# Moving weight loads, useless matmuls and small VectorE steps in the opening chain of a delta-rule attention with a gated MLP

## The chip, the core and the metric

The kernel runs on one core of a Trainium2 chip. The engines are TensorE (PE, with its weight loads shown as PEld), VectorE (DVE), ScalarE (ACT), GpSimd (POOL) and SyncE (SP, which issues the DMAs here). The metric is the device time of one execution in microseconds (us), as the median of several runs.

## The reference

Two parts follow each other. The first is a delta-rule attention with 4 batches, 8 heads, 768 tokens and 48 dimensions a head. Each of the 32 units keeps a 48 x 48 state, which every token reads and changes:

```python
k_n = k / (np.linalg.norm(k, axis=-1, keepdims=True) + 1e-06)
for t in range(S):
    kt, vt, bt = (k_n[:, :, t], v[:, :, t], beta[:, :, t, None])
    y[:, :, t] = np.einsum('bhd,bhde->bhe', q[:, :, t], state)
    v_old = np.einsum('bhde,bhd->bhe', state, kt)
    state = state + bt[:, :, :, None] * np.einsum('bhd,bhe->bhde', kt, vt - v_old)
```

The second is a gated MLP on the 3072 tokens, with 384 model dimensions and 1536 hidden ones: `sigmoid(x @ w_gate) * (x @ w_val) @ w_out`. All is float32.

## The kernel before

**Chunks.** The 768 tokens are worked in 12 chunks (g = 0 to 11) of 64 tokens, all 32 units at once, so a chunk gives 256 rows to the MLP. In a chunk the token-by-token recurrence becomes a triangular system: Gram matrices of k (`gram`), the norms of k from their diagonal (`norms`, 18 small DVE steps), the inverse of the triangular blocks (`solve_halves` for chunks 0 to 2, some 40 small DVE steps), products of q and k under a mask (`masked`), and then, in three steps, the new values (`updates(g, 0..2)`). In step 0 PE forms pu, and ACT and DVE copy it to su; step 1 adds to pk on PE, and `less` subtracts pk from the values on DVE (line 457); step 2 is like step 0. `rows` makes the chunk's outputs yy and copies them to ys, `flip` transposes them to xx for the MLP, and `advance` changes the state.

**The MLP.** Its hidden dimension is cut into 12 tiles (f). A slot is half a tile: in an even slot `gate_val` (line 583 for chunk 0) puts gate and value products of one tile into one of two PSUM buffers called gv, and `gated` frees it again (ACT's sigmoid, line 591, and DVE's product, line 592); in odd slots `outp` (line 611) works on the tile two before. The 36 weight pieces of 384 KB come in the order in which chunk 0 needs them: gate and value of tile 0, then for each further tile its gate and value and the output piece of the tile before. A piece n is loaded as two words a weight (`load_piece`, line 172), changed in place by two ACT instructions (`scaled`, lines 189 and 191), and joined to float32 by one on DVE (`join`, line 203). When `scaled(n)` is done, piece n + BEHIND is loaded, from piece EAGER = 14 on; the pieces before are issued by `stage`.

**The order** is written out by hand: each engine works in the order in which the program issues, and SP issues DMAs in that order too, so that a load which waits holds back those behind it. Ahead of slot 0 the program spells out the opening chain of chunk 0, in which nothing of the MLP can run. In the slots two tables, `plan` and `late`, say what is issued ahead of and behind a slot's own work. Piece 13 and piece 14 are scaled in slot 0, ahead of tile 0's sigmoid.

**Useless matmuls.** `busy_array` (line 99) issues matmuls of 128 x 512 in bf16 whose result nobody reads. In `solve_halves` of chunk 0, those at `pz` wait each for one of DVE's solving steps (`beats`); others stand between the chain's products under the names early, pm and gap.

Of the kernel before, what the change touches and what calls it, by code (L numbers as in the profile page):

```python
# [12 lines left out]
F32 = mybir.dt.float32  # L13
# [6 lines left out]
ALU = mybir.AluOpType  # L20
# [4 lines left out]
C = 64  # L25
# [5 lines left out]
J = 8  # L31
# [24 lines left out]
def deltanet_gated_mlp(ctx: ExitStack, tc: tile.TileContext, kd, qd, kv, beta, words, out):  # L56
# [39 lines left out]
    def busy_array(out, n, after=()):  # L96

        for i in range(n):
            ins = nc.tensor.matmul(out=out.rearrange("q a b -> q (a b)"), lhsT=flat[:, 0:128], rhs=flat, start=True, stop=True)
            if i < len(after):  # L100
                pace(ins, after[i])

    def load_k(g):
        for e in range(2):
            nc.sync.dma_start(kqp[g % 2][64 * e:64 * e + D, 0:2].rearrange("p s c t -> p (s c t)"), kd[g, e])

    def load_q(g, after=None):
        for e in range(2):
            ins = nc.sync.dma_start(kqp[g % 2][64 * e:64 * e + 64, 2 + e:4 + e].rearrange("p s c t -> p (s c t)"), qd[g, e])
            pace(ins, after)  # L110

    def load_rows(g, part):

        st = state[g]
        if "kv" not in st:
            st["kv"] = wk.tile([128, 2, CP, D], F32, name=f"kv_{g}", tag="kv", bufs=2)
        nc.sync.dma_start(st["kv"][:, part].rearrange("p c d -> p (c d)"), kv[g, :, part * CP * D:(part + 1) * CP * D])
        if part:
            st["beta"] = wk.tile([128, 32], F32, name=f"beta_{g}", tag="beta", bufs=2)
            nc.sync.dma_start(st["beta"], beta[:, g])  # L120
# [54 lines left out]
    def stage(lo, hi, after=None):  # L175
        for n in range(lo, hi):
            load_piece(n, after)
# [177 lines left out]
    def lower_left(g):  # L355

        if g == 0:
            for r in range(4):
                q, o = slice(32 * r, 32 * r + 32), 32 * (r % 2)
                nc.scalar.activation(wide[q, :, o:o + 16].rearrange("q c t -> q t c"), state[g]["G"][q, 0:16], AF.Copy, scale=under[q])  # L360
            return
        a = joints[g][:, 0]
        return nc.scalar.activation(a[:, :, 0:16].rearrange("q c t -> q t c"), state[g]["G"][:, 0:16], AF.Copy, scale=under)
# [9 lines left out]
    def solve_halves(g):  # L373


        st = state[g]
        gp, gam = st["gp"], st["gam"]
        X = st["X"]
        hg = wk.tile([128, 768], F32, name=f"hg_{g}", tag="hg", bufs=1)
        H = hg[:, 0:256].rearrange("q (b k t) -> q b k t", b=2, k=8)  # L380
        gs = hg[:, 256:768].rearrange("q (b i t) -> q b i t", b=2, i=16)
        for b in range(2):
            nc.vector.tensor_tensor(out=H[:, b], in0=dmask[:, 8 * b:8 * b + 8, 16 * b:16 * b + 16],
                                    in1=gam[:, 16 * b:16 * b + 16].unsqueeze(1).to_broadcast([128, 8, 16]), op=ALU.mult)
            yield
            nc.vector.scalar_tensor_tensor(out=gs[:, b], in0=gp[:, 16 * b:16 * b + 16, 16 * b:16 * b + 16], scalar=-1.0,
                                           in1=gam[:, 16 * b:16 * b + 16].unsqueeze(1).to_broadcast([128, 16, 16]), op0=ALU.mult, op1=ALU.mult)
            yield
        for j in range(15, 0, -1):
            k, n = j // 2, 8 - j // 2  # L390
            tmp = wk.tile([128, 2, n, j], F32, name=f"tmp_{g}_{j}", tag="tmp", bufs=2)
            beat(nc.vector.tensor_tensor(out=tmp, in0=H[:, :, k:8, j:j + 1].to_broadcast([128, 2, n, j]),
                                         in1=gs[:, :, j:j + 1, 0:j].to_broadcast([128, 2, n, j]), op=ALU.mult))
            yield
            beat(nc.vector.tensor_tensor(out=H[:, :, k:8, 0:j], in0=H[:, :, k:8, 0:j], in1=tmp, op=ALU.add))
            yield
        for b in range(2):
            nc.vector.tensor_copy(out=X[:, 8 * b:8 * b + 8, 16 * b:16 * b + 16], in_=H[:, b])
            yield
        A, D, Z = (joints[g][:, i] for i in range(3))  # L400
        nc.vector.transpose(mt.rearrange("q c (k r) -> q k c r", r=2), X.rearrange("q k (c r) -> q k c r", r=2))
        yield
        pool, tag = (ps_aux, "aux") if g else (ps_gv, "gv")
        pz, pm = (pool.tile([128, CP, 32], F32, name=f"{n}_{g}", tag=tag) for n in ("pz", "pm"))

        def blocks(out, lhsT, rhs):
            for c in range(CP):
                for r in range(0, 128, 32):
                    nc.tensor.matmul(out=out[r:r + 32, c], lhsT=lhsT[r:r + 32, c], rhs=rhs[r:r + 32, c], start=True, stop=True)  # L409
        if g == 0:  # L410
            paced = beats[8::2]
            busy_array(pz, len(paced) + 4, after=paced)
        if g:
            blocks(pz, A, mt)
        else:
            for c in range(CP):
                for r in range(0, 128, 64):
                    nc.tensor.matmul(out=pz[r:r + 64, c], lhsT=wide[r:r + 64, c], rhs=mt[r:r + 64, c], start=True, stop=True)
        if g == 0:
            busy_array(pm, 2)  # L420
        yield
        nc.vector.transpose(D.rearrange("q c t -> q (c t)"), mt.rearrange("q c t -> q (c t)"))
        nc.scalar.copy(Z, pz)
        yield
        blocks(pm, D, Z)
        if g == 0:
            gap.append(ps_gv.tile([128, J, C], F32, name="gap", tag="gv"))
            busy_array(gap[0], 3)
        yield
        st["joint"] = nc.vector.tensor_tensor(out=mt, in0=mt, in1=pm, op=ALU.subtract)  # L430
        yield
# [22 lines left out]
    def less(g):  # L454
        st = state[g]
        for e in range(2):
            nc.vector.tensor_tensor(out=st["R"][e], in0=st["kv"][:, 1, e * J:(e + 1) * J], in1=st["pk"][e], op=ALU.subtract)  # L457

    def updates(g, step):

        st = state[g]
        R, L = st["R"], st["L"]

        at = {(e, x): [tokens_at(e, x) + 32 * (k ^ e) for k in range(2)] for e, x in KINDS}
        if step == 1:
            for j in range(J):
                for e, x in KINDS:
                    one, two = at[e, x]
                    nc.tensor.matmul(out=st["pk"][e][two:two + 32, j], lhsT=L[one:one + 32, e * J + j], rhs=su[one:one + 32, 3 if x else e, j],  # L469
                                     start=False, stop=True, skip_group_check=True)  # L470
            less(g)
            return
        pu = [ps_aux.tile([128, J, D], F32, name=f"pu_{g}_{step}_{x}", tag="aux") for x in range(1 if g else 2)]
        for j in range(J):
            for e, x in KINDS:
                r = at[e, x][step // 2]
                nc.tensor.matmul(out=pu[0 if g else x][r:r + 32, j], lhsT=mt[r:r + 32, e * J + j], rhs=R[e][r:r + 32, j], start=True, stop=True)  # L477
        for e, x in KINDS:
            r = at[e, x][step // 2]
            if g == 0 and x:  # L480
                nc.vector.tensor_copy(out=su[r:r + 32, 3 if x else e], in_=pu[1][r:r + 32])
            else:
                nc.scalar.copy(su[r:r + 32, 3 if x else e], pu[0][r:r + 32])  # L483
# [168 lines left out]
    def take(gen, n=1):  # L652
        for _ in range(n):
            next(gen, None)
# [5 lines left out]
    scalings = [scale_v(g) for g in range(N)]  # L660
    NORMS, SOLVE, HALVES = 18, 66, 40
    joins, splits = joining(), splitting()
    EAGER, BEHIND = 14, 6


    EN = mybir.EngineType
# [12 lines left out]
    take(gram(0), 10)  # L679
    rest(0)  # L680
    masks0 = masked(0)
    gap.append(ps_gv.tile([128, J, C], F32, name="early", tag="gv"))
    busy_array(gap.pop(), 12)
    for n in range(2):
        scaled(n)
    for _ in norms(0):
# [8 lines left out]
        scaled(n)  # L695
    take(norms1, 11)
    take(halves0, 2)
    stage(10, 12, state[0]["joint"])
    load_q(1, state[0]["joint"])
    clear(1)  # L700
    take(masks0, 2)
    updates(0, 0)
    busy_array(gap[0], 5)
    stage(12, 14, lower_left(1))
    load_rows(1, 0)
    load_k(2)
    for n in range(6, 9):
        scaled(n)
    take(masks0, 2)
    updates(0, 1)  # L710
    busy_array(gap[0], 4)
    take(norms1, NORMS)
    updates(0, 2)
    busy_array(gap[0], 5)
    for n in range(9, 11):
        scaled(n)
    take(joins, 2)
    take(halves1, 4)
    rows(0)
    busy_array(gap[0], 2)  # L720
    for n in range(11, 13):
# [6 lines left out]
    for n, at in enumerate((0, 0, 1, 2, 3, 5, 6, 8, 9, 10, 10, 11, 11, 12, 12, 13, 14, 15, 16, 16, 17, 18, 18), 13):  # L728
        plan[at].append(lambda n=n: scaled(n))
    spread(joins, len(pieces) - 4, 0, 20)  # L730
    for at, n in ((0, 8), (1, 4), (2, 6), (3, 4), (4, 5), (5, 5), (6, 1), (9, 1), (11, 1)):
        plan[at].append(steps(halves1, n))
    plan[10].insert(0, steps(halves1))
    late[10].append(steps(halves1))
# [147 lines left out]
```

## Time and profile before

| | us |
|---|---|
| median of 3 runs | 636.92 (636.85 to 637.29) |
| the profiled execution | 635.61 |
| its span, first to last instruction | 633.9 |
| PE busy in the span | 614.6 |
| DVE busy | 476.8 |
| ACT busy | 344.0 |
| first gate product of tile 0 begins (line 583) | 42.09 |

The span is that of the instructions in the trace; 1.7 us of the execution lie around it. Times within the trace count from the start of the span. Where a row has an engine's name with a q, it is the engine's sequencer, which issues DMAs or waits; in the rows of stretches the last three numbers are the granted clock of TensorE, the busy share of the DMA engines and what these moved in GB/s.

### The profile page before, as it was taken

Reading aid. Unit: us, or ns where it says so; the run is one execution under the profiler, and the core shown is the slowest. Engines: PE = TensorE matmul, PEld = TensorE weight load, DVE = VectorE, ACT = ScalarE, POOL = GpSimd, SP = SyncE. Lnnn points to the kernel's source line nnn. Section 1 sums busy time; section 2 is a strip of 40 time slices with the busy share of each in tenths; the row PEclk is TensorE's granted clock in tenths of the full one; section 3 lists DMA queues with packets and bytes.
Section 4 is the critical chain, followed back from the end, with each engine's and each line's share of the span. In section 5 each row is a group of like instructions: output and inputs, shape, how many; then the busy total and the mean of one; then the engine's idle time right before and its main releaser. Section 6 shows DMA issues by size and latency. Waiting matters only on the chain.

```text
span 633.9 us, 24057 instructions
## 1 busy us (share of the span) xinstructions
PE 614.6 (97%) x10494; PEld 571.2 (90%) x10502; DVE 476.8 (75%) x1443; ACT 344.0 (54%) x933; POOL 39.6 (6%) x102
## 2 busy tenths in 40 slices
PE   6689999999999999999999999999999999999996
PEld 4367778989999999999999999999999999999996
DVE  5888897589977977977977977977987977953221
ACT  4879865567356356356355355355455455445222
POOL 6000000000002002002002002002002002001000
PEclk9999999999999999999999999999999999999999
DMA  9495831202203203103102102102112100100101
GB/s 271 177 296 181 277 91 54 53 2 87 52 3 86 52 4 86 42 12 86 45 11 86 34 21 87 27 28 86 26 29 86 26 4 3 26 3 2 26 1 25
DMA packets 17769, 41.06 MB, mean 65 GB/s; under 512 B 4224, under 2 KB 7296, under 8 KB 17664
## 3 DMA queue, kind: packets, MB, share of 16 engines
q1 hardware_dynamic: 17664, 39.53, 21.5%
q8 instruction: 82, 1.34, 0.9%
q14 instruction: 23, 0.19, 0.1%
HBM read 34.80 MB, written 4.72 MB: 62 GB/s over the span
## 4 chain that ended last, share of the span: by engine, by line
PE 91%; DVE 5%; ACT 1%; issue 1%; DMA 1%; ACTq 0%; SPq 0%; DVEq 0%
PE gv L586 45%; PE po L617 22%; PE gv L583 5%; PE pu L477 3%; PE po L611 3%; PE yy L503 2%; PE yy L506 2%; PE pk L446 2%; PE pg L291 2%; PE pp L319 2%; PE pd L524 2%; PE pk L469 1%; PE pm L409 1%; ACT su L483 1%; DVE kqp L324 1%
## 5 line engine op out<-in xcount | busy, mean ns | idle before, releaser
L586 PE MATMUL gv<-xx,w 128*128 128x256 f32 x2376 | 311.2, 285 | 0.0
L586 PEld LDWEIGHTS gv<-xx,w 128*128 128x128 f32 x2376 | 298.8, 191 | 3.1
L617 PE MATMUL po<-w,h 128*128 128x384 f32 x792 | 161.9, 340 | 0.0
L617 PEld LDWEIGHTS po<-w,h 128*128 128x128 f32 x792 | 133.8, 188 | 0.8
L597 ACT CAST h<-sg 128x256 fp32r<-128x256 f32 x132 | 53.5, 405 | 120.1 <-DVE sg L592 119.0
L591 ACT ACTIVATE sg<-gv 128x256 f32<-128x256 f32 x144 | 54.7, 380 | 107.8 <-PE gv L586 98.5
L592 DVE TENSOR_TENSOR sg<-sg,gv 128x256 f32<-128x256 f32 x144 | 60.1, 417 | 67.3 <-ACT sg L591 66.5
L350 DVE TENSOR_TENSOR X<-X,tmp 128x126 f32<-128x126 f32 (+22 forms) x279 | 71.1, 255 | 8.3
L347 DVE TENSOR_TENSOR tmp<-X,gp 128x126 f32<-128x126 f32 (+22 forms) x279 | 71.0, 254 | 8.3
L602 DVE TENSOR_TENSOR h<-sg,h 128x256 fp32r<-128x256 f32 x132 | 56.4, 428 | 13.2 <-ACT h L597 13.2
L562 POOL COPY x<-yt 32x192 f32<-32x192 f32 x72 | 28.3, 393 | 450.3 <-DVE yt L557 447.6
L279 ACT ACTIVATE kv<-kv,mq 128x48 f32<-128x48 f32 x192 | 47.9, 324 | 0.0
L483 ACT COPY su<-pu 32x384 f32<-32x384 f32 x92 | 43.3, 470 | 5.9 <-PE pu L477 4.1
L583 PE MATMUL gv<-xx,u 128*128 128x256 f32 x144 | 33.8, 385 | 0.7 <-issue 0.4
L324 DVE TENSOR_TENSOR kqp<-pp,pmask 64x512 f32<-64x512 f32 x48 | 32.3, 687 | 2.1 <-PE pp L319 1.1
L303 ACT COPY G<-pg 32x256 f32<-32x256 f32 (+1 forms) x69 | 25.3, 367 | 14.0 <-PE pg L291 12.7
L583 PEld LDWEIGHTS gv<-xx,u 128*128 128x128 f32 x144 | 26.6, 190 | 5.8 <-issue 0.8
L557 DVE STREAM_TRANSPOSE yt<-ys 128x768 f32<-128x768 f32 x9 | 8.8, 979 | 25.4 <-ACT ys L512 25.4
L457 DVE TENSOR_TENSOR R<-kv,pk 128x384 f32<-128x384 f32 x44 | 22.3, 549 | 6.6 <-PE pk L469 6.5
L562 ACT COPY x<-yt 32x192 f32<-32x192 f32 x72 | 25.2, 349 | 1.2
L212 ACT CAST w<-u 128x384 fp32r<-128x384 f32 x36 | 18.0, 508 | 8.1 <-DVE w L219 8.0
L531 DVE TENSOR_TENSOR su<-su,pd 48x384 f32<-48x384 f32 x40 | 21.7, 543 | 0.8 <-PE pd L524 0.4
(109 smaller groups left out, 556.2 us busy)
## 6 DMA issues: line engine op xcount, KB each, us to landing
raw<-in_words_dram SPq DMA_DIRECT2D x36, 384.0 KB, 5.5
kv<-in_kv_dram SPq DMA_DIRECT2D x24, 384.0 KB, 4.5
kqp<-in_qd_dram SPq DMA_DIRECT2D x24, 256.0 KB, 4.1
kqp<-in_kd_dram SPq DMA_DIRECT2D x24, 192.0 KB, 3.5
out_dram<-ot SPq DMA_DIRECT2D x48, 96.0 KB, 2.2
beta<-in_beta_dram SPq DMA_DIRECT2D x12, 16.0 KB, 4.0
```

The source lines that it names most:

```text
L279: nc.scalar.activation(V[:, c], V[:, c], AF.Copy, scale=mq[:, c, 0:1])
L347: nc.vector.tensor_tensor(out=tmp, in0=X[:, k:16, j:j + 1].to_broadcast([128, n, j]), in1=gp[:, j:j + 1, 0:j].to_broadcast([128, n, j]), o ...
L350: nc.vector.tensor_tensor(out=X[:, k:16, 0:j], in0=X[:, k:16, 0:j], in1=tmp, op=ALU.add)
L483: nc.scalar.copy(su[r:r + 32, 3 if x else e], pu[0][r:r + 32])
L562: copy(x[32 * q:32 * q + 32, :, :, a].rearrange("q k c s -> q c k s"), yt[32 * a:32 * a + 32, :, q::4])
L583: nc.tensor.matmul(out=pg[:, o], lhsT=parts[w, f][:, k * 128:(k + 1) * 128], rhs=x[0][:, k], start=k == 0, stop=k == KC - 1)
L586: nc.tensor.matmul(out=pg[:, o], lhsT=parts[w, f][:, a, k * 128:(k + 1) * 128], rhs=x[b][:, k], start=(k == 0 and q == 0), stop=(k == KC - ...
L591: nc.scalar.activation(h, st["gv", f][:, 0], AF.Sigmoid)
L592: nc.vector.tensor_tensor(out=h, in0=h, in1=st["gv", f][:, 1], op=ALU.mult)
L597: nc.scalar.copy(hh[:, 0], st["sg", f])
L602: nc.vector.tensor_tensor(out=hh[:, 1], in0=st["sg", f], in1=hh[:, 0].bitcast(F32), op=ALU.subtract)
L617: nc.tensor.matmul(out=po[s], lhsT=hh[:, a, ts], rhs=parts["o", f][:, w], start=(f == 0 and q == 0), stop=(f == NF - 1 and q == 2))
```

## The change

Six things are done at once, all ahead of slot 4 of the MLP:

- The 12 useless matmuls "early" go, four of those at pz, and one of two at pm.
- Pieces 10 to 13 are issued together when the subtraction of `updates(0, 1)` is done. Before, 10 and 11 waited for the subtraction of mt in `solve_halves` (line 430), and 12 and 13 for the ACT instruction of `lower_left(1)` (line 363). The k of chunk 2, the q of chunk 1 and the k rows of chunk 1 follow them.
- BEHIND is 5 instead of 6, so piece 14 follows `scaled(9)`.
- The second pair of chunk 0's masks stands behind the subtraction of `updates(0, 1)` instead of ahead of it, and the rest of chunk 1's norms behind the copies of `updates(0, 2)`.
- The joins of pieces 0 and 1 stand ahead of the first copies to su, instead of behind `updates(0, 2)`.
- The first four steps of `solve_halves` of chunk 1 are no longer ahead of `rows(0)`; slots 1, 2 and 3 take 6, 7 and 5 steps for 4, 6 and 4.

```diff
         if g == 0:
             paced = beats[8::2]
-            busy_array(pz, len(paced) + 4, after=paced)
+            busy_array(pz, len(paced), after=paced)
...
         if g == 0:
-            busy_array(pm, 2)
+            busy_array(pm, 1)
...
     def less(g):
         st = state[g]
         for e in range(2):
-            nc.vector.tensor_tensor(out=st["R"][e], in0=st["kv"][:, 1, e * J:(e + 1) * J], in1=st["pk"][e], op=ALU.subtract)
+            last = nc.vector.tensor_tensor(out=st["R"][e], in0=st["kv"][:, 1, e * J:(e + 1) * J], in1=st["pk"][e], op=ALU.subtract)
+        return last
...
-            less(g)
-            return
+            return less(g)
...
-    EAGER, BEHIND = 14, 6
+    EAGER, BEHIND = 14, 5
...
     masks0 = masked(0)
-    gap.append(ps_gv.tile([128, J, C], F32, name="early", tag="gv"))
-    busy_array(gap.pop(), 12)
     for n in range(2):
         scaled(n)
...
     take(halves0, 2)
-    stage(10, 12, state[0]["joint"])
-    load_q(1, state[0]["joint"])
     clear(1)
     take(masks0, 2)
+    take(joins, 2)
     updates(0, 0)
     busy_array(gap[0], 5)
-    stage(12, 14, lower_left(1))
-    load_rows(1, 0)
-    load_k(2)
+    lower_left(1)
     for n in range(6, 9):
         scaled(n)
+    stage(10, 14, updates(0, 1))
+    load_k(2)
+    load_q(1)
+    load_rows(1, 0)
+    busy_array(gap[0], 4)
     take(masks0, 2)
-    updates(0, 1)
-    busy_array(gap[0], 4)
-    take(norms1, NORMS)
     updates(0, 2)
     busy_array(gap[0], 5)
+    take(norms1, NORMS)
     for n in range(9, 11):
         scaled(n)
-    take(joins, 2)
-    take(halves1, 4)
     rows(0)
...
-    for at, n in ((0, 8), (1, 4), (2, 6), (3, 4), (4, 5), (5, 5), (6, 1), (9, 1), (11, 1)):
+    for at, n in ((0, 8), (1, 6), (2, 7), (3, 5), (4, 5), (5, 5), (6, 1), (9, 1), (11, 1)):
```

SP's queue from piece 10 to piece 14 before (raw_552 and raw_554 are pieces 10 and 11, raw_606 and raw_608 are 12 and 13, raw_619 is 14; kqp_77 takes the q of chunk 1, kqp_76 the k of chunk 2, kv_113 the k rows of chunk 1):

```order
L172 DMA raw_552<-in_words_dram 128x768
L172 DMA raw_554<-in_words_dram 128x768
L109 DMA kqp_77<-in_qd_dram 64x1024 x2
L172 DMA raw_606<-in_words_dram 128x768
L172 DMA raw_608<-in_words_dram 128x768
L117 DMA kv_113<-in_kv_dram 128x768
L105 DMA kqp_76<-in_kd_dram 48x1024 x2
L172 DMA raw_619<-in_words_dram 128x768
```

And now (raw_625 to raw_631 are pieces 10 to 13, raw_698 is piece 14):

```order
L172 DMA raw_625<-in_words_dram 128x768
L172 DMA raw_627<-in_words_dram 128x768
L172 DMA raw_629<-in_words_dram 128x768
L172 DMA raw_631<-in_words_dram 128x768
L105 DMA kqp_76<-in_kd_dram 48x1024 x2
L109 DMA kqp_77<-in_qd_dram 64x1024 x2
L117 DMA kv_113<-in_kv_dram 128x768
L172 DMA raw_698<-in_words_dram 128x768
```

The same nine transfers stand ahead of piece 14; the four pieces come first among them, and all of them stand behind one wait.

DVE from the subtraction of mt (line 430) on, before (L324 are the masks, L481 the copies to su, L457 is the subtraction in `less`, L259 a step of the norms):

```order
L430 TENSOR_TENSOR mt<-mt,pm_406 128x512
L324 TENSOR_TENSOR kqp_76<-pp_0_208,pmask 64x512 x2
L481 COPY su<-pu_0_1_563 32x384 x2
L324 TENSOR_TENSOR kqp_76<-pp_1_209,pmask 64x512 x2
L457 TENSOR_TENSOR kv_92<-kv_92,pk_0_204 128x384
L457 TENSOR_TENSOR kv_92<-kv_92,pk_1_205 128x384
L259 TENSOR_TENSOR nt_470<-nt_470,gp_466 128x32
```

And now (L203 are the joins of pieces 0 and 1):

```order
L430 TENSOR_TENSOR mt<-mt,pm_393 128x512
L324 TENSOR_TENSOR kqp_76<-pp_0_208,pmask 64x512 x2
L203 SCALAR_TENSOR_TENSOR u_538<-raw_98 128x384
L203 SCALAR_TENSOR_TENSOR u_538<-raw_100 128x384
L481 COPY su<-pu_0_1_542 32x384 x2
L457 TENSOR_TENSOR kv_92<-kv_92,pk_0_204 128x384
L457 TENSOR_TENSOR kv_92<-kv_92,pk_1_205 128x384
L324 TENSOR_TENSOR kqp_76<-pp_1_209,pmask 64x512 x2
L481 COPY su<-pu_2_1_645 32x384 x2
```

Two joins stand ahead of the first copies to su, and the second pair of masks and the norms stand behind the subtraction and the second copies.

## The prediction

> **What bounds the kernel now.** I read the page first, the shares of the chain that ended last by engine:
>
> ```profile
> PE 91%; DVE 5%; ACT 1%; issue 1%; DMA 1%; ACTq 0%; SPq 0%; DVEq 0%
> ```
>
> PE is the bound for nearly all of the span. So the change can act in two ways: it moves the moment when PE starts its dense work, or it makes PE wait after that. Then I read the same chain in order of time (start, length, what).
>
> ```profile
> 23.80 2.07 PE pz L418 x64
> ...
> 26.53 1.50 PE pm L409 x100
> ...
> 28.82 0.86 PE pu L477 x59
> 29.68 1.31 issue
> ...
> 42.09 5.42 PE gv L583 x24
> ...
> 49.33 2.79 PE gv L583 x12
> ...
> 53.40 2.59 PE gv L583 x12
> ...
> 71.22 0.42 issue
> ```
>
> Up to 42.09 us a serial chain of the first chunk passes between DVE, PE and ACT. From 42.09 on the chain is PE alone: tiles 0 and 1 of the gate and value products (24 matmuls), tile 2 at 49.33, tile 3 at 53.40. The row at 29.68 is a stall of 1.31 us inside 64 small matmuls, with nothing to wait for.
>
> **The stall in pu.** It is an instruction fetch, as three rows of the page bear out.
>
> ```profile
> PE 614.6 (97%) x10494; PEld 571.2 (90%) x10502; DVE 476.8 (75%) x1443; ACT 344.0 (54%) x933; POOL 39.6 (6%) x102
> q8 instruction: 82, 1.34, 0.9%
> ```
>
> 10494 and 10502 instructions of PE over 82 packets are 256 a packet. In program order (an f32 matmul is two loads and two multiplies) the stalls at 29.68 and 71.22 stand 1536 instructions apart, six times 256. So a block can be late when PE uses 256 instructions fast: here pm and pu, some 375 in 3 us.
>
> By the Trainium skill, "Runtime: NRT & Kernel Launch", section "Instruction fetch mechanics", blocks are indeed 256 instructions, but fetch is hidden; by that rule the shift below would be worth nothing. The 1.31 us row disagrees.
>
> The change takes 34 PE instructions out ahead of this place (12 + 4 + 1 useless matmuls of two each). The block's end moves 34 further on: out of pu, 14 instructions into pk (L469). PE reaches pk only when the su copies are done, so the block has landed by then. The block before it now ends some 34 instructions deeper in pm, and its fetch is asked for later: 0 to 0.55 us of stall there; I take 0.2, since the 32 instructions that delay the request are handed on faster than they execute.
>
> **What DVE does with that.** DVE's rows in order of time:
>
> ```profile
> 28.08 0.69 DVE L430 TENSOR_TENSOR mt<-mt,pm 128x512 f32<-128x512 f32 x1 [0.23 <-PE pm L409]
> 28.80 1.39 DVE L324 TENSOR_TENSOR kqp<-pp,pmask 64x512 f32<-64x512 f32 x2
> 31.32 1.14 DVE L481 COPY su<-pu 32x384 f32<-32x384 f32 x2 [1.13 <-PE pu L477]
> 32.49 1.40 DVE L324 TENSOR_TENSOR kqp<-pp,pmask 64x512 f32<-64x512 f32 x2
> 33.92 1.02 DVE L457 TENSOR_TENSOR kv<-kv,pk 128x384 f32<-128x384 f32 x2
> ...
> 36.50 1.14 DVE L481 COPY su<-pu 32x384 f32<-32x384 f32 x2
> 37.67 1.03 DVE L203 SCALAR_TENSOR_TENSOR u<-raw 128x384 uint32<-128x384 uint32 x2
> ```
>
> and PE's row between them:
>
> ```profile
> 32.39 0.99 PE L469 MATMUL pk<-su,L 32*32 32x48 f32 x64
> ```
>
> The change puts two word joins (1.03) behind the first two masks. The stall that leaves pu was the cover of just that slot (1.13 idle). So: subtraction of mt ends 28.97, masks 30.36, joins 31.4, su copies 32.55 (before 32.46): nothing gained so far. Then pk ends at 33.5, and the subtraction L457 starts there instead of behind two more masks (33.92): it ends at 34.6, against 34.94. The masks follow, 1.40, and the next su copies start at 36.0 instead of 36.50, since the norms' seven steps have moved behind them. The block setup of chunk 1 no longer stands ahead of the ys copy. ACT's last copy of xx waits for pieces 10 to 12, so the first gv matmul comes at 41.6: **-0.5 us** for the chain (bounds -0.75, by DVE alone, and +0.3, if piece 12 lands 0.8 late). The useless matmuls taken out of this stretch were not in it: pz waits for DVE's mt and pm for ACT's copy.
>
> **What the loads cost.** Here is SP's own order before (start, length of the issues):
>
> ```profile
> 28.79 1.00 SPq L172 DMA_DIRECT2D raw<-in_words_dram  x2
> 29.84 1.11 SPq L109 DMA_DIRECT2D kqp<-in_qd_dram  x2
> 33.02 1.39 SPq L172 DMA_DIRECT2D raw<-in_words_dram  x2
> 34.45 0.44 SPq L117 DMA_DIRECT2D kv<-in_kv_dram  x1
> 34.98 0.85 SPq L105 DMA_DIRECT2D kqp<-in_kd_dram  x2
> 35.92 19.10 SPq L172 DMA_DIRECT2D raw<-in_words_dram  x11
> ```
>
> and what waits for the first of those eleven, piece 14:
>
> ```profile
> 44.99 0.56 ACT L189 ACTIVATE raw<-raw 128x384 int32<-128x384 uint16 x1 [2.35 <-DMA raw<-in_words_dram]
> ...
> 45.89 0.36 ACT L591 ACTIVATE sg<-gv 128x256 f32<-128x256 f32 x1
> 46.28 0.42 DVE L592 TENSOR_TENSOR sg<-sg,gv 128x256 f32<-128x256 f32 x1 [1.65 <-ACT sg L591]
> ...
> 47.35 0.23 DVE L395 TENSOR_TENSOR hg<-hg,tmp 128x66 f32<-128x66 f32 x1
> 47.61 0.22 DVE L392 TENSOR_TENSOR tmp<-hg 128x60 f32<-128x60 f32 x1
> ...
> 50.41 0.42 DVE L592 TENSOR_TENSOR sg<-sg,gv 128x256 f32<-128x256 f32 x1
> ```
>
> On ACT the scaling of piece 14 stands ahead of the first sigmoid. ACT waits 2.35 us for its landing at 44.99; the gated product of tile 0 ends at 46.70, 1.71 later, that of tile 1 at 50.83, DVE having worked without a break between them (4.13). These free the two PSUM buffers for tiles 2 and 3, which PE starts at 49.33 and 53.40. So before there are 2.6 us of slack in both, and that is what hides the loads.
>
> The same nine transfers stand ahead of piece 14 after the change, but the first is issued at 34.6 instead of 28.79: 5.8 us later, for data of which ACT was already short. What gives some back is the order: four pieces together, then the narrow transfers. The answer on the word loads from 28 to 50 us has the time from issue to landing, and the stretches have the rates (last number, GB/s; DMA share ahead of it):
>
> ```profile
> DMA to landing us min/median/max: 3.0/5.4/9.0
> 10.00:15.00 5.00, 4.67 (x35) 1.88 (x33) 4.49 (x22) 2.38 (x6) 0.96 (x4) 1.00 1.04 314
> 15.00:20.00 5.00, 2.60 (x69) 1.36 (x62) 4.31 (x21) 4.77 (x11) 0.00 (x0) 1.00 1.04 398
> 37.00:41.00 4.00, 2.99 (x71) 2.42 (x72) 3.91 (x11) 3.57 (x9) 0.00 (x0) 1.00 0.95 230
> ```
>
> Piece 10 lands 3.0 after its issue (the smallest landing), at 37.6. Pieces 11 to 13, 1.18 MB at the 398 of pure pieces: 40.6. Then k, q, kv and piece 14, 1.70 MB, at the 230 of the stretch that carried such transfers before: 48.0. Ends: 46.0, with the 314 of the early mixture for the second part; 50.8, with the 218 GB/s that all nine had before (2.88 MB from 31.8 to 44.99). I take 48.0, nearest to the same transfers beside the same engines' work.
>
> From there: tile 0's product ends at 49.7, and tile 2 starts at 49.8 (+0.5). DVE then has three more steps of the next chunk's solve ahead of tile 1's product (13 for 10, one each 0.25 us: 4.13 + 0.75 = 4.9), which ends at 54.6: tile 3 at **54.7, +1.3 us** against 53.40. At the ends of the landing: -0.5 (then the chain's gain decides) and +4.1. Behind tile 3 the later products have their slack again (they keep the distance to ACT and DVE, which run without a break there), and PE does not make up lost time. So this +1.3 takes the place of the -0.5; they are not added.
>
> **The rest.** The fetch stall of 0.42 at 71.22 goes: its block end moves from the tile-6 matmuls into pu of chunk 1, behind the next output product. The following block then ends near the close of chunk 1's masks and can be late by up to 0.5: together -0.3 (-0.6 to +0.2). Pieces behind 14 come one scaling later; the late ones lay 2 to 6 us in hand, so nothing. SP's queue holds the later inputs of chunk 2 in the same places.
>
> **Sum:** 1.3 - 0.3 = +1.0 us. The profiled execution took 635.61 (span 633.9 and 1.7 around it), which makes 636.6; the median of the runs is 1.31 above that execution, so I carry the difference over: 636.92 + 1.0 = **637.9 us**.
>
> **Rivals.** (1) *The transfers run cleanly* and piece 14 lands by 46: the chain's gain stays, -0.5 - 0.3, **636.1**, down to 635.1 with the best ends. For it: 398 GB/s when pieces run alone. Against: 230 in the same place before. It decides below a landing of 46.2. (2) *A cold array.* The useless matmuls show two speeds (smallest, median and largest ns; first and last start):
>
> ```profile
> L99 PE MATMUL pz<-dmask x14: 379/389/390, 17.8 to 23.1; 128*128 128x512 bf16 x14
> L99 PE MATMUL early<-dmask x11: 379/634/634, 10.6 to 14.5; 128*128 128x512 bf16 x11
> 4.92 1.98 PE L291 MATMUL pg<-kqp 48*64 48x64 f32 x62 [0.59 <-DMA kqp<-in_kd_dram]
> 14.76 1.16 PE L291 MATMUL pg<-kqp 48*64 48x64 f32 x64
> ```
>
> The array sped up while "early" ran; 5.4 us of small matmuls before that had not done it. Without "early" it falls to the eleven paced ones, one per 0.5 us from 17.78. If these don't suffice, pz runs 1.98/1.16 x 64/62 = 1.76 times as long, +1.6, and if the array stays slow to 42 us, pz, pm, pu and pk alone (5.4 us by the rows above) cost +4.1, and what follows, as an estimate, 2 more. With a part of the loads' cost: **639.5 to 645, 642** in the middle. For: nothing dense is left before 17.8. Against: at a slow length of 0.634, with starts 0.39 apart as in "early" (ten in 3.9 us), the paced ones, one each half microsecond, still fill some 80% of 4.9 us. The Trainium skill, "TensorE: Matmul & The Clock Gate", Part 1, says that the clock is released after one busy window of about 3.4 us, and that the windows are not tied to the start of the kernel; by it the eleven would do in most executions, not in all. The rows of "early", slow at first and fast within 3.9 us, agree. (3) *Nothing moves*: landing near 47, and losses and gains cancel, **636.9**.
>
> **Chances.** Forecast 0.52 (637.0 to 640.5), rival 1 0.22, rival 2 0.13, rival 3 0.13. A measurement of this kernel tells about 0.2%, 1.3 us, from no change. Slower by more, over 638.2: three fifths of the forecast, whose bounds reach further up than down, and rival 2 whole, 0.44. Faster by more: two thirds of rival 1, with what I may have missed in the chain, 0.15. Within: 0.41. The range reaches into rival 1 and the cheap half of rival 2: 635.4 to 641.5.
>
> **What would show it.** Right: no stall in pu; subtraction L457 ends near 34.6; ACT waits 5 us or more ahead of the first sigmoid; PE idle ahead of tiles 2 and 3; none at tile 6. Wrong: piece 14 landing before 46.5, PE without a break from 42 us on, or useless matmuls of 634 ns late in the pz group.

## The result, and the profile after

The change made the kernel slower: **639.81 us** (median of 6 runs, 639.12 to 640.66) against 636.70 (median of 6 runs beside them, 635.33 to 637.29); ratio 1.0061, 95% interval 1.0049 to 1.0073. Ratios here leave disturbed runs out and so need not be the quotient of the medians. The profiled execution after took 640.00 us (span 638.3), the one before 635.61 (633.9): the two profiles differ by 4.4 us, the medians by 3.1, and the steps below are read from the profiles.

The shares of the chain that ended last, after:

```profile
PE 85%; DVE 3%; ACT 3%; DMA 1%; issue 1%; SPq 1%; ACTq 0%
```

Before, PE had 91% and ACT 1%. What has come in stands in the same chain in order of time (start, length, what):

```profile
36.19 0.33 SPq L172
...
40.77 9.37 DMA raw<-in_words_dram
...
50.17 0.56 ACT raw L189
...
53.91 0.46 ACT raw L191
54.36 0.35 ACT su L529
...
64.06 0.39 ACT sg L591
...
64.81 1.49 DVE u L203 x3
...
70.67 0.72 DVE scratch L422
...
71.52 1.28 PE pm L409 x80
```

Piece 10 is issued at 36.19 and piece 14 at 40.77; it lands at 50.15. From there the chain lies on ACT's queue for 14 us, then on DVE's, and reaches PE only at 71.52, in the pm product of chunk 1's solve (`solve_halves(1)`). PE's rows in order of time, after:

```profile
23.80 3.60 PE L418 MATMUL pz<-mt,wide 64*64 64x32 f32 x64 [1.14 <-DVE mt L401]
...
28.07 1.93 PE L409 MATMUL pm<-scratch 32*32 32x32 f32 x128
...
31.04 0.88 PE L477 MATMUL pu<-kv,mt 32*32 32x48 f32 x64
...
43.42 5.45 PE L583 MATMUL gv<-xx,u 128*128 128x256 f32 x24 [0.87 <-ACT xx L545]
...
51.93 2.86 PE L583 MATMUL gv<-xx,u 128*128 128x256 f32 x12 [1.25 <-DVE sg L592]
...
56.76 2.86 PE L583 MATMUL gv<-xx,u 128*128 128x256 f32 x12 [0.68 <-DVE sg L592]
...
71.52 1.28 PE L409 MATMUL pm<-scratch 32*32 32x32 f32 x128 [1.38 <-DVE scratch L422]
...
74.12 2.75 PE L583 MATMUL gv<-xx,u 128*128 128x256 f32 x12
```

and tile 3 and the last of these places before:

```profile
53.24 2.75 PE L583 MATMUL gv<-xx,u 128*128 128x256 f32 x12
...
66.38 1.62 PE L409 MATMUL pm<-scratch 32*32 32x32 f32 x128
...
69.33 1.89 PE L583 MATMUL gv<-xx,u 128*128 128x256 f32 x8
71.64 1.13 PE L583 MATMUL gv<-xx,u 128*128 128x256 f32 x4 [0.42 <-issue]
```

So PE is behind by 1.33 us at tile 0 (42.09 before), by 3.5 at tile 3 (53.24 in this view before), and by **5.1** at chunk 1's pm, for which it now waits 1.38; tile 6 then takes 2.75 instead of 3.44 without its fetch stall, and 4.4 are left at the end. The stall in pu is gone: 0.88 in one row at 31.04. On DVE the subtraction L457 ends at 36.17, and ACT waits 5.24 us for piece 14:

```profile
35.15 1.02 DVE L457 TENSOR_TENSOR kv<-kv,pk 128x384 f32<-128x384 f32 x2 [0.98 <-issue]
50.17 0.56 ACT L189 ACTIVATE raw<-raw 128x384 int32<-128x384 uint16 x1 [5.24 <-DMA raw<-in_words_dram]
```

And pz took 3.60 us for 2.06, under a halved clock (stretches; the columns that matter are PE busy, and at the end the granted clock, DMA share and GB/s):

```profile
20.45:23.86 3.41, 1.96 (x9) 0.52 (x9) 2.95 (x13) 3.39 (x15) 0.09 (x1) 1.00 0.47 179
23.86:30.69 6.83, 6.70 (x195) 5.58 (x196) 4.26 (x13) 4.10 (x12) 0.44 (x1) 0.50 0.02 5
```

Two causes were on the table at once, then: late words, and the half-speed stretch of rival 2.

### The profile page after: what moved, and what is told of

Its sections match the earlier page's. It is cut to its first block, busy times and chain, and to the rows that moved or that the text cites. A ratio compares the mean times of both kernels' runs of the same rounds, so it can differ in the third digit from the quotient of the medians.

```text
span 638.3 us, 24030 instructions
## 1 busy us (share of the span) xinstructions
PE 615.4 (96%) x10485; PEld 572.5 (90%) x10485; DVE 476.9 (75%) x1443; ACT 344.3 (54%) x933; POOL 39.6 (6%) x102
## 4 chain that ended last, share of the span: by engine, by line
PE 85%; DVE 3%; ACT 3%; DMA 1%; issue 1%; SPq 1%; ACTq 0%
PE gv L586 44%; PE po L617 21%; PE gv L583 3%; PE pu L477 3%; PE po L611 2%; PE yy L503 2%; PE yy L506 2%; PE pp L319 2%; PE pk L446 2%; DMA raw<-in_words_dram 1%; PE pg L291 1%; PE pd L524 1%; PE pk L470 1%; ACT su L483 1%; ACT raw L189 0%
## 5 line engine op out<-in xcount | busy, mean ns | idle before, releaser
L602 DVE TENSOR_TENSOR h<-sg,h 128x256 fp32r<-128x256 f32 x132 | 56.4, 428 | 13.2 <-ACT h L597 13.2
L324 DVE TENSOR_TENSOR kqp<-pp,pmask 64x512 f32<-64x512 f32 x48 | 32.3, 686 | 2.0 <-PE pp L319 1.1
L457 DVE TENSOR_TENSOR R<-kv,pk 128x384 f32<-128x384 f32 x44 | 22.3, 549 | 6.4 <-PE pk L470 6.4
L189 ACT ACTIVATE raw<-raw 128x384 int32<-128x384 uint16 x36 | 20.0, 557 | 7.0 <-DMA raw<-in_words_dram 7.0
L291 PE MATMUL pg<-kqp 48*64 48x64 f32 x768 | 16.2, 235 | 7.8 <-DMA kqp<-in_kd_dram 7.8
```

Source lines behind the costliest of these rows:

```text
L602: nc.vector.tensor_tensor(out=hh[:, 1], in0=st["sg", f], in1=hh[:, 0].bitcast(F32), op=ALU.subtract)
```

## The experiments

The theories, as the expectations use them. **A**: the moment at which the words land costs; ACT's and DVE's in-order queues carry the lateness to PE. **B**: the half-speed array costs. **C**: the new order of joins, masks and norms on DVE costs. Each ratio below is against the kernel before on the same chip (medians there 635.4 to 636.0).

### One of the three parts undone, or done alone

`loads_back`, after with the loads of before:

```diff
+    stage(10, 12, state[0]["joint"])
+    load_q(1, state[0]["joint"])
...
+    stage(12, 14, lower_left(1))
+    load_rows(1, 0)
+    load_k(2)
...
-    stage(10, 14, updates(0, 1))
+    updates(0, 1)
...
-    EAGER, BEHIND = 14, 5
+    EAGER, BEHIND = 14, 6
```

> The changed kernel with the loads of pieces 10 to 13, k, q and k rows issued where they were before, and BEHIND 6 again; fewer useless matmuls and the new order of the small steps stay. Theory A (late words set everything from tile 2 on): piece 14 lands near 45 us, tiles 2 and 3 start near 49.3 and 53.4 again, and about 636 to 637 us are measured; the array may still be slow in pz, but that is hidden or small. Theory B (the array's half-speed stretch is the cost): the stretch stays, since nothing dense is put back, and 639 us or more stay. Theory C (the new order of joins, masks and norms on DVE costs): 639 us or more stay too, with a full-speed clock.

Measured: 635.14 us, ratio 0.9987 (0.9971 to 1.0003). The whole loss is gone, with the half-speed stretch still there (24.48 to 31.30).

`fillers_back`, after with the useless matmuls of before:

```diff
+    gap.append(ps_gv.tile([128, J, C], F32, name="early", tag="gv"))
+    busy_array(gap.pop(), 12)
...
-            busy_array(pz, len(paced), after=paced)
+            busy_array(pz, len(paced) + 4, after=paced)
...
-            busy_array(pm, 1)
+            busy_array(pm, 2)
```

> The changed kernel with the useless matmuls of before (12 early, 4 more at pz, 2 at pm). Theory B: the granted clock stays full from some 14 us on, pz takes 2.06 us again, the subtraction L457 ends 1.5 us earlier, and the time falls by about 1.5 to 2 us to 638 us. Theory A: PE's chain and the loads move, but the late words stay; 638.5 to 640. A third reading, from the six runs of the changed kernel (granted clock .993, .993, .995, .996, .999, .999 with 639.1, 639.3, 640.0, 639.6, 640.4, 640.7 us): the runs with the slow stretch are the quicker ones, so that a full clock does not help or costs up to 1: 640 to 641.

Measured: 640.07 us, ratio 1.0060 (1.0040 to 1.0080). The clock stayed full through the first chain and pz took 2.06 us, yet nothing came back: the third reading. Theory B falls as an account of the loss.

`order_back`, after with the small steps of DVE in their old places (the edits of the change at `take(masks0, 2)`, `take(norms1, NORMS)`, `take(joins, 2)`, `take(halves1, 4)` and the table undone).

> The changed kernel with the masks, norms, joins and the first steps of chunk 1's solve in the places of before; the new loads and the fewer useless matmuls stay. Theory C: the time falls by 1 us or more, towards 638 or less. Theory A: the subtraction L457 ends 0.5 to 1 us later behind the masks, the loads with it, so the same or up to 1 us slower: 639.8 to 641. Theory B: the same as the changed kernel, 639.8, with a half-speed stretch.

Measured: 640.05 us, ratio 1.0062 (1.0041 to 1.0082). Theory C falls.

`loads_only`, before with the loads of after alone.

> The kernel before with only the loads moved (pieces 10 to 13, k, q and k rows behind the subtraction of updates(0, 1), BEHIND 5). Theory A: all of the loss is here: piece 14 lands near 48 to 50 us, tiles 2 and 3 start 1.3 to 3.5 us later, 638.5 to 640. Theory B: the clock stays full, so no more than the loads' own 0 to +1: 636.7 to 637.7. Theory C: 636.7.

Measured: 641.18 us, ratio 1.0073 (1.0048 to 1.0099), more than A expected. Here, as in `fillers_back`, PE waited longer ahead of tile 0 (1.94 us here), which cost a second time. The stretches of `fillers_back`:

```profile
41.02:44.44 3.42, 0.91 (x5) 0.51 (x4) 3.28 (x11) 1.95 (x6) 0.00 (x0) 1.00 1.04 221
44.44:47.85 3.41, 3.41 (x10) 2.70 (x9) 0.00 (x0) 0.94 (x2) 0.00 (x0) 0.50 1.02 285
```

and its tiles 0 and 1 among PE's rows:

```profile
43.88 7.13 PE L583 MATMUL gv<-xx,u 128*128 128x256 f32 x24 [2.51 <-ACT xx L545]
```

PE waited 2.51 us for ACT's copy of xx, which stood behind the scaling of piece 12 (landed 42.45); the clock halved for the next 3.41 us, and the 24 matmuls took 7.13 instead of 5.42, in `loads_only` too. This does not hide a gain of `fillers_back`: its pm of chunk 1 started at 71.25, when ACT's and DVE's queues let it (table below), 0.27 us ahead of the changed kernel.

`order_only`, before with only the new order.

> The kernel before with only the masks, norms, joins and first solve steps of chunk 1 in their new places. By the prediction's second term: the joins fill the gap that the stall in pu leaves, L457 ends 0.3 us earlier, the first gate product 0.2 to 0.5 us earlier, loads as before: 0 to -0.5, so the same by measurement. Theory C (the new order itself costs): 1 us slower or more.

Measured: 635.84 us, ratio 1.0003 (0.9991 to 1.0015): no difference, as by the prediction's second term.

So the loads are the whole of it: of the kernels above, each with the new loads lost 0.6 to 0.7%, and the two without them nothing.

### Which part of the loads

`loads_early`: the four pieces still in one lump and BEHIND 5, but behind the subtraction of mt.

```diff
     take(halves0, 2)
+    stage(10, 14, state[0]["joint"])
...
-    stage(10, 14, updates(0, 1))
+    updates(0, 1)
```

> The changed kernel with pieces 10 to 13 still issued together and with BEHIND 5, but behind the subtraction of mt (L430, about 30 us) instead of behind the subtraction L457 (about 35). Theory A (the moment of the issue is what costs): piece 12 lands by 38, piece 14 by 46, tiles 0, 2 and 3 start within 0.5 us of the kernel before, 635.5 to 636.5. Theory A2 (four pieces in one lump, the narrow loads behind them, and BEHIND 5 are what costs): piece 14 still lands near 50 and 639 to 640 stay.

Measured: 635.70 us, ratio 1.0005 (0.9992 to 1.0018). Issued at 30.4 instead of 36.2, the lump costs nothing (piece 14 landed at 45.46): the moment is what costs, not the order or BEHIND.

`narrow_later`: the loads at the late moment, but k, q and k rows behind piece 17.

```diff
     stage(10, 14, updates(0, 1))
-    load_k(2)
-    load_q(1)
-    load_rows(1, 0)
...
     flip(0, 1)
     busy_array(gap[0], 2)
+    load_k(2)
+    load_q(1)
+    load_rows(1, 0)
```

> The changed kernel with the k of chunk 2, the q and the k rows of chunk 1 issued behind piece 17 instead of between pieces 13 and 14; pieces 10 to 13 still wait for the subtraction L457, at about 36 us. Theory A (what costs is when pieces 12, 14 and 15 land; in seven profiles chunk 1's pm started 19.1 to 19.3 us behind the end of the scaling of piece 15): piece 12 lands by 41, piece 14 by 44, the scaling of piece 15 ends near 46.5, chunk 1's pm starts without a wait, and 635.5 to 637 us are measured. Theory A3 (the wait behind L457 itself costs, whatever follows): 639 or more.

Measured: 638.16 us, ratio 1.0054 (1.0032 to 1.0075): missed. Piece 14 landed at 43.80 and chunk 1's pm did not wait, as expected; but the k of chunk 2 was now late itself. PE's rows of this kernel:

```profile
49.12 0.33 PE L291 MATMUL pg<-kqp 48*64 48x64 f32 x2 [1.15 <-DMA kqp<-in_kd_dram]
50.05 1.16 PE L291 MATMUL pg<-kqp 48*64 48x64 f32 x62 [0.59 <-DMA kqp<-in_kd_dram]
```

The Gram products of chunk 2 ended at 51.20 (49.33 before), 1.9 us late. Later PE stalled 0.84 us inside chunk 1's pm, with nothing to wait for. This kernel's runs spread widely, from 636.46 to 642.32 us.

`k_in_place`: as `narrow_later`, but with the k of chunk 2 left behind piece 13.

> The changed kernel with only the q and the k rows of chunk 1 issued behind piece 17; the k of chunk 2 stays behind piece 13. With all three moved, piece 14 landed at 43.8 us instead of 50.2 and chunk 1's pm did not wait, but the Gram products of chunk 2 (line 291) waited 1.1 us for that k and ended 2 us late. Theory A (only the landings count, each at the product that needs it): piece 14 lands at 45 to 47, the Gram products start without a wait, chunk 1's pm starts within 0.5 us of 66.4 and waits 0.5 at most, and 635.5 to 636.7 us are measured. Theory A3 (issuing behind L457 costs by itself): 638 or more.

Measured: 638.97 us, ratio 1.0046 (1.0031 to 1.0060): missed again, and this miss tells most. The time is the one that theory A3 gave, but the trace shows another cause than the place of the issue. Piece 14 landed at 45.72, and PE ran from 42.03 to 66.41 without a break, as in the kernel before. Then, in ACT's rows:

```profile
50.60 0.56 ACT L189 ACTIVATE raw<-raw 128x384 int32<-128x384 uint16 x1 [1.02 <-DMA raw<-in_words_dram]
51.05 0.54 ACT L191 ACTIVATE raw<-raw 128x384 f32<-128x384 f32 x1
```

and in PE's:

```profile
68.75 1.34 PE L409 MATMUL pm<-scratch 32*32 32x32 f32 x128 [2.34 <-DVE scratch L422]
70.03 2.93 PE L611 MATMUL po<-u,sg 128*128 128x384 f32 x4
```

Piece 17, the last of four that ACT scales before it turns to chunk 1, landed at 50.58. ACT's queue and then DVE's follow without a break to the transpose of line 422, and chunk 1's pm starts a fixed time behind the end of that scaling:

| | piece 14 lands | piece 17 scaled | chunk 1's pm starts | difference | PE waited |
|---|---|---|---|---|---|
| before | 44.97 | 49.24 | 66.38 | 17.14 | 0 |
| `loads_early` | 45.46 | 49.71 | 66.83 | 17.12 | 0 |
| `loads_back` | 44.42 | 50.05 | 67.18 | 17.13 | 0.47 |
| `k_in_place` | 45.72 | 51.59 | 68.75 | 17.16 | 2.34 |
| `order_back` | 47.63 | 51.89 | 68.99 | 17.10 | 2.12 |
| `fillers_back` | 49.88 | 54.13 | 71.25 | 17.12 | 1.31 |
| `loads_only` | 50.04 | 54.31 | 71.43 | 17.12 | 1.72 |
| after | 50.15 | 54.36 | 71.52 | 17.16 | 1.38 |

(All in us, each from that kernel's trace.) The kernel before is already at this limit: PE shows no wait there, and yet the difference is the same to within 0.06 us, so that PE and DVE's transpose come at one moment. So a later landing shows in full at this place. An earlier one does not: in `block_shift` (below) piece 17 was scaled at 48.79, 0.45 us earlier, and pm started at 66.32, 17.53 later, as PE came no sooner. That a gain in the first chain alone would be hidden in the same way follows from the table, but no run shows it.

### The queue itself

`words_later`: the loads of after, with ACT's scalings put behind what PE needs first.

```diff
-    for n in range(11, 13):
+    for n in range(11, 12):
         scaled(n)
...
     flip(0, 1)
     busy_array(gap[0], 2)
+    scaled(12)
...
-    for n, at in enumerate((0, 0, 1, 2, 3, 5, 6,
+    for n, at in enumerate((0, 3, 3, 3, 4, 5, 6,
```

> The changed kernel with all its loads where they are, but ACT scales piece 12 behind its copies of xx, and pieces 14 to 16 behind the sigmoid of tile 1. Theory A1 (nobody needs these words so early; it is the instructions queued behind the waiting one on ACT that come late): tile 0 starts near 42, tiles 2 and 3 start with no gap or under 0.5 us, the wait ahead of chunk 1's pm shrinks, and 636 to 637.5 us are measured. Theory A0 (the words themselves are short, the transfers are the bound): the wait moves to the joins and to tiles 4 to 6, and 639 or more stay.

Measured: 639.58 us, ratio 1.0063 (1.0051 to 1.0075). Theory A1's time was missed. The waits ahead of tiles 2 and 3 are gone, but they only add up at the next place (PE):

```profile
49.86 2.86 PE L583 MATMUL gv<-xx,u 128*128 128x256 f32 x12
...
53.85 2.75 PE L583 MATMUL gv<-xx,u 128*128 128x256 f32 x12
...
71.03 1.53 PE L409 MATMUL pm<-scratch 32*32 32x32 f32 x128 [3.52 <-DVE scratch L422]
72.49 2.92 PE L611 MATMUL po<-u,sg 128*128 128x384 f32 x4
```

`words_turn`: the same, with DVE's transpose of mt for chunk 1 right behind the one that makes mt.

```diff
         nc.vector.transpose(mt.rearrange(...), X.rearrange(...))
+        if g:
+            nc.vector.transpose(D.rearrange(...), mt.rearrange(...))
         yield
...
-        nc.vector.transpose(D.rearrange(...), mt.rearrange(...))
+        if g == 0:
+            nc.vector.transpose(D.rearrange(...), mt.rearrange(...))
         nc.scalar.copy(Z, pz)
```

> The kernel with the words scaled later, and in it DVE's transpose of mt for chunk 1 (line 422) directly behind the transpose that makes mt (line 401) instead of behind five steps of the norms. With the words scaled later alone PE ran without a break to 67.5 us and then waited 3.5 us for this transpose ahead of chunk 1's pm. Theory Q (the place in DVE's and ACT's queues is what PE waits for): the wait falls by 2 to 2.4 us, to ACT's copy of pz at about 68.7, and the time from 639.6 to 637.2 to 637.8. Theory W (something else is late by the same amount, the pieces themselves): the wait only moves to a later product, 639 or more.

Measured: 637.21 us, ratio 1.0025 (1.0008 to 1.0042), where `words_later` had 639.58. In this kernel pm is line 411 and the copy of pz line 426:

```profile
68.40 1.29 PE L411 MATMUL pm<-scratch 32*32 32x32 f32 x128 [1.24 <-ACT scratch L426]
```

The wait fell by 2.28, and the releaser is now ACT's copy of pz: theory Q. What PE waits for is a place in two in-order queues, not the words, which are used later.

### The instruction fetch, and an attempt at a quicker kernel

`block_shift`: before with 9 useless matmuls early, 2 more at pz and 1 at pm (for 12, 4 and 2).

> The kernel before with six useless matmuls fewer (three of the twelve early, two at pz, one at pm), which moves the end of the instruction block 12 further on, out of pu, while the granted clock stays full. Fetch theory: no stall in pu, su copies and the subtraction L457 about 1.1 us earlier, the first gate product 0.5 to 1.1 earlier, 635.1 to 636.4 if what follows keeps up; no gain in the time (0 to -0.3) if DVE and ACT, busy without a break from 42 us on, hold PE back at chunk 1's pm. No-fetch theory: the stall of 1.31 stays where it was, before the same product, and the time too.

Measured: 635.45 us, ratio 1.0001 (0.9987 to 1.0015). Its chain in order of time:

```profile
28.75 0.88 PE pu L477 x64
29.63 0.32 PE gap L99
29.96 0.74 issue
...
33.73 0.79 PE pu L477 x54
34.52 1.55 issue
36.07 0.30 PE pu L477 x8
```

The stall left the first pu (0.74 us of it stayed among the useless matmuls behind), and DVE's L457 started 1.26 us earlier (32.66 for 33.92). One block later PE stalled for 1.55 us in the second pu, and tile 0 began at 42.05, as before.

`combined`: before with 15 useless matmuls fewer, the norms and first solve steps of chunk 1 later, piece 12 scaled behind the copies of xx, and the early transpose of `words_turn`.

> An attempt at a quicker kernel: the loads of the kernel before; 15 useless matmuls fewer (all twelve early, one at pz, two at pm), so that both block ends leave the two pu products; the norms and first solve steps of chunk 1 behind the second copies to su, the masks where they were; piece 12 scaled behind the copies of xx; chunk 1's transpose of line 422 directly behind line 401. If the fetch stalls of the first chain (1.3 us in the first pu before, 1.8 in the second where only the first was removed) are gone and nothing after 42 us holds PE back: first gate product at 40.5 to 41.2, and 634.0 to 635.2 us where the kernel before takes 635.7. If the stall moves to a third block end, or piece 14 and ACT's queue hold PE back as before: 635.2 to 636.

Measured: 634.92 us against 635.42, ratio 0.9994 (0.9979 to 1.0009): not told from no change. In the profiled execution (636.28 us, above the median) tile 0 began at 43.65 instead of the expected 40.5 to 41.2. Its chain has the stall one block further on still, ahead of yy:

```profile
35.06 0.32 PE gap L99
35.39 2.08 issue
37.47 1.04 PE gap L99 x4
```

## Why the prediction was right and wrong

The forecast was a loss by late loads, 637.9 us in a range of 635.4 to 641.5; 639.81 was measured. The sign and the cause hold: `loads_back` and `loads_early` lose nothing, and the rest of the change taken together is worth nothing (`loads_back`). The size was 2 us short, and these are the steps.

**The stall in pu** went, as predicted, and none came in pm in its place (0.2 had been allowed for): pm ran at half speed.

**DVE and the chain**: L457 was to end at 34.6 and ended at 36.17. The order was right (joins in the slot, masks behind); the half-speed stretch was not in the sum. pz took 3.60 / 2.06 = 1.75 times as long, which is rival 2's figure of 1.76. So rival 2's mechanism happened together with the forecast's: in all eight profiles of kernels with the change's useless matmuls the array fell to half speed between 23.9 and 25.8 us. With all the useless matmuls of before it fell in one profile of four, `order_only`, and there ahead of pz (19.64 to 23.05). The sign that rival 2 had named, matmuls of 634 ns late in the pz group, did not show: the last five took 389 to 396 ns, and the clock fell behind them. Tile 0 came at 43.42 instead of 41.6, since piece 12 landed at 42.00 and ACT scales it ahead of its copy of xx: the bound that the step named, further out. But rival 2's price was wrong: with the same stretch `loads_back` loses nothing, and with a full clock `fillers_back` is not quicker. The six executions after say so too: 639.1 and 639.3 us at a mean granted clock of 0.993, 640.4 and 640.7 at 0.999.

**The loads**: the step was right in its mechanism and nearly in size. From first issue to the landing of piece 14, 13.4 us were worked out and 13.96 measured; from the landing to tiles 2 and 3, 1.8 and 6.7 were worked out and 1.78 and 6.61 measured. What was off most is the start, 36.19 for 34.6, by the half-speed stretch: in `narrow_later`, where that began at 25.78, behind most of pz (2.12 us), the first issue was at 34.84. So tile 3 came 3.5 us late in the profile instead of 1.3.

**"Behind tile 3 the later products have their slack again"** is the step that failed. It looked at the gated products alone. Chunk 1's pm, behind tile 5, hangs on DVE's transpose, and this on 17.1 us of ACT and DVE without a break behind the scaling of piece 17. That place had no slack at all before (17.14 us in the table, as where PE waits), and there PE lost another 1.6 us in the profile, to 5.1. `k_in_place` shows it alone: nothing late at tiles 0 to 5, 2.34 us of wait at pm, and 638.97 us.

**The fetch at tile 6** was right: its stall went, and tile 6 took 0.69 us less (-0.3 taken, -0.6 the bound, so a little more than the bound).

**The other rivals**: clean transfers (1) and cancelling terms (3) did not come about; piece 14 landed 4 us behind the point from which rival 1 would have decided.

What stays open: why the same nine transfers and piece 14 took 13.2 us from the first issue in `order_back`, 13.96 after and 15.2 in `loads_only`. Part of it is SP's issuing: piece 14 was issued 4.6, 4.6 and 5.8 us behind piece 10, and landed 8.6, 9.4 and 9.4 us after its own issue. Open too is what each of the 3.1 us of the medians goes to, since only one execution of each kernel has a trace. The fewer useless matmuls were not tried alone (`block_shift` takes out 6 of the 17, and its time did not change).

## What to carry to other kernels

Where two engines work through in-order queues without a break, a late transfer is paid where their queues next meet the bounding engine, however far behind and whatever the slack in between: follow the queue to its end, not to the first product that has slack. Before moving loads later, list what stands behind each waiting instruction, and find the place with the least slack; here it lay 35 us behind the first late issue, with nothing in hand. And a place that is bound twice, by PE and by ACT's queue, can hide a gain on one of them alone, as `block_shift` shows for ACT's.

## What the runs showed that was not expected

**The clock falls after a window that is not idle.** The granted clock goes by windows of 3.41 us. Past 30 us in the fourteen profiles, the six full-speed windows in which PE was busy for 24 to 44% were each followed by one at half speed, and those with 50% or more were not. The two nearest to the edge, in `combined`:

```profile
35.55:38.96 3.41, 1.49 (x36) 0.83 (x36) 3.07 (x11) 2.22 (x6) 0.00 (x0) 1.00 1.02 334
38.96:42.38 3.42, 3.42 (x49) 2.58 (x42) 1.31 (x3) 1.36 (x3) 0.00 (x0) 0.50 1.03 245
```

and in `loads_only`:

```profile
68.18:71.60 3.42, 1.70 (x26) 1.19 (x28) 3.28 (x11) 3.42 (x10) 0.00 (x0) 1.00 0.86 244
```

The first halved the clock, the last did not. So a wait of 2.1 to 3.5 us costs twice: in `order_back`, `k_in_place` and `words_later` the output product behind pm took 2.9 us instead of 1.56; with waits of 1.2 to 1.7 (after, `fillers_back`, `loads_only`, `words_turn`) it did not. The Trainium skill, "TensorE: Matmul & The Clock Gate", Part 1, has the array fall back after an idle window of about 3.4 us; the length of the window agrees, but here 1.92 us without matmuls in a window were enough (the first row above). The useless matmuls paced at one per half microsecond did not hold the clock either, at 57% busy by the row of 20.45 above. So the busy share alone gives no threshold: ahead of 30 us windows at 54% (`order_only`) and 57% (after) were followed by half speed, and windows at 57 and 59% in the kernel before were not.

**Fetch stalls move on, they don't go.** Block ends taken out of one product stalled PE in the next block: 1.31 us before, 0.74 + 1.55 in `block_shift`, 2.08 in `combined`. The Trainium skill, "Runtime: NRT & Kernel Launch", section "Instruction fetch mechanics", has the fetch mostly hidden; in this chain of small matmuls it is not.
